# First layer of a four-layer kernel: v weights in two steps, output weights sooner, two scans in flight, norm row ahead of transposes, den steps moved

## The chip, the cores and the metric

One core of one Trainium2 chip. The metric is the device time of one execution in microseconds, the median of several runs. All runs compared here are of the fast state; the one run that fell into the slow state is named where it occurs.

## The reference

Four layers on 2048 rows of 1024 columns, in bfloat16: linear attention, gated product, and both again with the same weights. The attention layer is what the change touches.

```python
phi = lambda t: jnp.where(t > 0, t + 1, jnp.exp(t)) + 1e-6
pq, pk = phi(q), phi(k)                      # q, k, v = layernorm(x) @ wqkv, 32 heads of 32
kv  = jnp.einsum("bhsd,bhse->bhde", pk, v)
z   = jnp.einsum("bhsd->bhd", pk)
num = jnp.einsum("bhqd,bhde->bhqe", pq, kv)
den = jnp.einsum("bhqd,bhd->bhq", pq, z)[..., None] + 1e-6
...                                          # x = x + (num / den) @ wo
h   = (x @ w_gate) * (x @ w_up)              # gated layer, x = x + h @ w_down
```

## The kernel before

TensorE works almost all the time. In the first layer it makes keys, then queries interleaved with an x product (which takes the place of the v product), then folds `kv` with the output weights `wo`, and goes on to the gated layer. Beside this, ScalarE "scans" all gated-layer weights: 42 stripes of 128x2048 are fetched and their squares summed, for a scale that is needed only at the gated layer. Transfers are issued on three queues: SyncE's (transposes of the divided queries, weights of the next layer), GpSimd's (scan stripes from number 16 on) and ScalarE's (the v weights `wv` and `wo`, both 2 x 1 MB).

```python
wo = [ST[...], TX[...]]                     # both halves lie in buffers that query preparation used before
pqb = [...3 x W..., ...3 x MX...]           # six buffers for query tiles; the transpose of tile t frees one for tile t+6
def load_o():
    for n in range(2):
        nc.scalar.dma_start(out=wo[n], in_=wo_v[:, :, n * NB:(n + 1) * NB])
...
def scan_fetch():
    while scanned[1] < scanned[2]:
        i = scanned[1]
        if any(scan_buf[j] is scan_buf[i] for j in range(scanned[0], i)) or i >= max(EARLY, scanned[0] + 3):
            return
        (nc.sync if i < SYNC else nc.gpsimd).dma_start(out=scan_buf[i], in_=scan_src(i))
        scanned[1] += 1
...
def den_divide(t, pq, den):                 # last step of a query tile
    nc.vector.tensor_tensor(out=pqh, in0=pqh, in1=den..., op=ALU.mult)
    tx(pq, t, t // TPG)                     # dma_start_transpose on SyncE's queue
...
def kvo_unit(c):                            # needs wo; line 932 of the profile
    for n in range(2):
        nc.tensor.matmul(out=ps[:, n, :], lhsT=kvt[:, c, :], rhs=wo[n][:, c, :], start=True, stop=True)
    nc.scalar.activation(out=KVo[c], in_=ps, func=ACT.Copy, scale=rz[:, c:c + 1])
...
    scanned[2] = MID                        # MID = 32: from here scans up to 31 may be fetched
    scan_fetch()
    q(7, b0, 2)
    scan_step(1)
    q(8, a1, 1)
    scan_step(1)
    q(9, b1, 1)
    scan_step(1)
    q(10, b0, 2)
    load_o()
    scan_step(1)                            # scan 27, counted from 0
```

## Time and profile before

| | before |
|---|---|
| time, median of 3 runs | 1492.12 us |
| span of the profiled run | 1488.0 us |
| TensorE's waits in the first layer that the change aims at | 11.5 us |
| first matmul of the x products | 73.92 us |
| second half of `wo`: issued, landed | 165.14, 179.65 us |
| first matmul with that half | 179.70 us |
| first matmul with the sums in TX, gated layer | 256.33 us |

The rows from the fourth on are milestones: the times at which TensorE passes fixed places of the program. The difference of a milestone between two kernels tells what was won or lost up to there. The list of waits, the slow-clock stretches and the entry to the gated layer are shown in the prediction.

### The profile page before, as it was taken

The numbers are of one execution on the slowest core, as the hardware profiler recorded it, in microseconds if no ns is written. First come the engines' busy times: TensorE is split into PE (matmuls) and PEld (weight loads), VectorE is DVE, ScalarE is ACT, GpSimd is POOL, SyncE is SP. The second block draws the span as 40 slices with busy tenths as digits, with TensorE's granted clock in tenths as the row PEclk, the third lists the DMA queues.
The fourth block names the chain that finished last, engine by engine and source line by source line (L and its number), as shares of the span: only waits on it lengthen the run. The fifth ranks groups of instructions, "written<-read, shape, count | busy, mean of one in ns | idle before, by whom it ended". The sixth has DMA issues, their size and how long they took to land. (4 is left out here: it accounts for less than half of the span.)

```text
span 1488.0 us, 17649 instructions
## 1 busy us (share of the span) xinstructions
PE 1469.0 (99%) x6913; PEld 668.1 (45%) x6913; DVE 1056.5 (71%) x1577; ACT 744.5 (50%) x693; POOL 103.3 (7%) x230
## 2 busy tenths in 40 slices
PE   9899899999999999999999999999999999999999
PEld 3344444444444444444444445444444444444444
DVE  7676788988866477776479778867776845777532
ACT  6678687787700355550087347545563015566200
POOL 2201112000001000000042000200000100000000
PEclk9999999999999999999999999999999999999999
DMA  6466958697647333325739444353332753333442
GB/s 179 119 200 199 282 116 194 199 268 213 214 148 218 82 94 93 88 85 182 221 85 241 71 132 95 64 127 92 86 86 99 243 164 95 85 85 85 154 166 84
DMA packets 267443, 213.29 MB, mean 143 GB/s; under 512 B 102240, under 2 KB 250336, under 8 KB 263776
## 3 DMA queue, kind: packets, MB, share of 16 engines
q1 hardware_dynamic: 254352, 181.63, 43.3%
q0 software_dynamic: 6624, 24.12, 5.8%
q10 hardware_dynamic: 6384, 6.42, 1.3%
q8 instruction: 54, 0.88, 0.3%
q14 instruction: 29, 0.24, 0.1%
HBM read 162.59 MB, written 27.00 MB: 127 GB/s over the span
## 5 line engine op out<-in xcount | busy, mean ns | idle before, releaser
L1008 PEld LDWEIGHTS <-K 128*128 128x128 f16 x3136 | 306.8, 98 | 369.9 <-DVE TX L973 0.2
L1008 PE MATMUL Q<-XT,K 128*128 128x512 bf16 (+1 forms) x1792 | 405.7, 379 | 0.0
L1303 PE MATMUL Q<-K,K 128*128 128x512 f16 (+2 forms) x1582 | 340.4, 377 | 0.0
L1008 PE MATMUL Q<-TX,K 128*128 128x512 f16 x1344 | 308.4, 379 | 0.0
L970 ACT ACTIVATE K<-K,fac 128x2048 f16<-128x2048 bf16 x112 | 224.6, 2008 | 130.5 <-DMA K<-in_B_w_gate_dram 128.4
L1303 PEld LDWEIGHTS <-K 128*128 128x128 f16 x1582 | 154.3, 98 | 184.5
L973 DVE TENSOR_TENSOR K<-K 128x1024 f16<-128x1024 f16 (+1 forms) x244 | 157.3, 666 | 99.1 <-ACT K L970 96.5
L973 DVE TENSOR_TENSOR W<-MX,Q 128x1024 f16<-128x1024 f32 x88 | 107.4, 1220 | 37.4 <-PE Q L1008 18.6
L1028 ACT COPY MX<-Q 128x1024 f32<-128x1024 f32 x60 | 60.8, 1013 | 122.0 <-PE Q L1008 109.6
L973 DVE TENSOR_TENSOR W<-W,Q 128x1024 f16<-128x1024 f32 x80 | 97.6, 1220 | 17.7 <-PE Q L1008 13.2
L1028 ACT COPY W<-Q 128x1024 f32<-128x1024 f32 x52 | 52.6, 1012 | 89.8 <-PE Q L1008 77.3
L419 PE MATMUL Q<-K,K 128*128 128x512 bf16 x384 | 90.5, 391 | 5.1 <-DMA K<-ST 2.2
L973 DVE TENSOR_TENSOR K<-K,K 128x512 f16<-128x512 f16 (+1 forms) x148 | 87.7, 597 | 4.2
L419 PE MATMUL Q<-K,XT 128*128 128x512 bf16 x384 | 86.3, 379 | 1.0 <-DVE rz L464 0.5
L237 ACT ACTIVATE K<-K 128x2048 bf16<-128x2048 bf16 x42 | 79.9, 1907 | 5.4 <-DMA K<-in_B_w_down_dram 3.4
L1012 DVE TENSOR_TENSOR K<-W 128x512 f16<-128x512 f16 x168 | 71.3, 424 | 5.7
L1317 DVE SCALAR_TENSOR_TENSOR W<-Q,kap,X 128x1024 f32<-128x1024 f32 x16 | 20.5, 1284 | 65.7 <-PE Q L1303 65.7
L394 ACT ACTIVATE W<-Q 128x1024 bf16<-128x1024 f32 (+1 forms) x43 | 40.3, 940 | 49.4 <-PE Q L419 49.2
L297 DVE BATCH_NORM_STATS2 st<-X 128x6 f32<-128x512 bf16 x98 | 62.0, 674 | 3.0 <-DMA X<-in_A_x_dram 2.9
L1025 ACT COPY MX<-Q 128x1024 f32<-128x1024 f32 x28 | 28.3, 1009 | 70.2 <-PE Q L1008 57.3
L419 PEld LDWEIGHTS <-K 128*128 128x128 bf16 x384 | 38.0, 100 | 54.4 <-DMA K<-K 5.5
L303 POOL TENSOR_SCALAR ve<-mv 128x1 f32<-128x1 f32 x48 | 12.4, 258 | 704.9 <-DVE mv L301 704.5
(198 smaller groups left out, 1379.5 us busy)
## 6 DMA issues: line engine op xcount, KB each, us to landing
K<-WD SPq DMA_DIRECT2D x28, 1792.0 KB, 7.4
K<-in_B_w_gate_dram SPq DMA_DIRECT2D x70, 512.0 KB, 4.1
K<-in_B_w_up_dram SPq DMA_DIRECT2D x58, 512.0 KB, 5.2
K<-in_A_wqkv_dram SPq DMA_DIRECT2D x8, 1024.0 KB, 6.9
WZ<-K POOLq DMA_DIRECT2D x16, 512.0 KB, 7.0
K<-in_B_w_down_dram POOLq DMA_DIRECT2D x14, 512.0 KB, 6.9
K<-in_B_w_up_dram POOLq DMA_DIRECT2D x12, 512.0 KB, 5.0
K<-in_B_w_down_dram SPq DMA_DIRECT2D x10, 512.0 KB, 5.6
```

The lines of the kernel that those rows point to most:

```text
L237: nc.scalar.activation(out=scan_buf[i], in_=scan_buf[i], func=ACT.Square, accum_out=acc[:, m, c:c + 1])
L297: nc.vector.bn_stats(out=stat[t][0][:, c, :], in_=X[:, t, c * NB:(c + 1) * NB])
L394: nc.scalar.activation(out=e, in_=ps, func=ACT.Exp)
L419: nc.tensor.matmul(out=ps, lhsT=xt[:, k, tl * P:(tl + 1) * P], rhs=w[:, k, :], start=(k == 0), stop=(k == KD - 1))
L970: nc.scalar.activation(out=b.bitcast(F16), in_=b, func=ACT.Copy, scale=fac[:, m:m + 1])
L973: eng.tensor_tensor(out=o, in0=a, in1=b, op=op)
L1008: nc.tensor.matmul(out=pair[:, m, :], lhsT=stationary(n, p, m, k), rhs=moving[p][:, k, :], start=(p in (1, 2, 5) and k == 0), stop=(k == K ...
L1012: nc.vector.tensor_tensor(out=hA[i][:, u, :], in0=gu[:, 0, :], in1=gu[:, 1, :], op=ALU.mult)
L1025: nc.scalar.copy(out=snaps[u, 1], in_=a)
L1028: nc.scalar.copy(out=snaps[u, p], in_=a)
L1303: nc.tensor.matmul(out=ps_[:, lo:hi], lhsT=act[:, u, j * P:(j + 1) * P], rhs=w[:, u, lo:hi], start=(p in (1, 2, 5) and u == 0), stop=(u == ...
L1317: stt(out=o, in0=ps_, scalar=kap[:, 0:1], in1=x, op0=ALU.mult, op1=ALU.add)
```

## The change

Intent: take away TensorE's short waits in the first layer. The output weights are issued two query tiles sooner; the v weights come in two steps, which costs scans 18 to 23 two of their four buffers; only two scans are kept in flight; the one-column norm row is read back ahead of two transposes; and a small product (`z_column`) with its denominators is moved from query 4 to query 9.

```diff
-    scan_buf = [scan_a[i % 4] for i in range(EARLY)] + [scan_c[i % 4] for i in range(NSCAN - EARLY)]
+    scan_buf = [scan_a[i % 4 if i < 18 else 2 + i % 2] for i in range(EARLY)] + [scan_c[i % 4] for i in range(NSCAN - EARLY)]
...
-            if any(...) or i >= max(EARLY, scanned[0] + 3):
+            if any(...) or i >= max(EARLY, scanned[0] + 2):
...
-            if i in (EARLY - 3, EARLY - 1):
-                n = (i - EARLY + 3) // 2
+            if i in (18 - 1, EARLY - 1):
+                n = (i + 1) // EARLY
                 nc.scalar.dma_start(out=wv[n], in_=wqkv_v[...])
...
-        q(3, b0, 2)
+        q(3, b0, 3)
...
         q(4, a0, 3)
-        at_pair(b0)
-        z_column()
...
         q(8, a1, 1)
+        load_o()
         scan_step(1)
+        at_pair(a0)
+        z_column()
         q(9, b1, 1)
         scan_step(1)
-        q(10, b0, 2)
-        load_o()
+        q(10, b0, 1)
...
                 elif i == 3:
                     nc.sync.dma_start(out=WS[:, :], in_=part[:, 3:4])
-                elif i == 6:
+                elif i == 4:
                     nc.sync.dma_start(out=row, in_=WS[:, :].rearrange("p o -> o p").to_broadcast([P, P]))
-                elif i == 8:            # norm from the row
+                elif i == 9:
-                elif i == 9:            # key scale
+                elif i == 10:
```

More of the change, by code (lines that the diff above doesn't have):

```diff
@@ L226, in scan_fetch @@
             i = scanned[1]
-            if any(scan_buf[j] is scan_buf[i] for j in range(scanned[0], i)) or i >= max(EARLY, scanned[0] + 3):
+            if any(scan_buf[j] is scan_buf[i] for j in range(scanned[0], i)) or i >= max(EARLY, scanned[0] + 2):
                 return
```

## The prediction

> **What bounds the kernel now.** I read the page first: TensorE is busy nearly the whole span, so only its idle time and its slow-clock time can be won. The first row is TensorE's share; the second block is the list of what TensorE waited for (engine and line, releaser: us in total, times, longest).
>
> ```profile
> PE 1469.0 (99%) x6913; PEld 668.1 (45%) x6913; DVE 1056.5 (71%) x1577; ACT 744.5 (50%) x693; POOL 103.3 (7%) x230
> ...
> PE Q L932 <- DMA TX<-in_A_wo_dram: 5.3, 1, 5.3
> PE Q L419 <- DMA K<-ST: 2.2, 1, 2.2
> PE Q L419 <- ACT W L408: 1.9, 2, 1.7
> ...
> PE Q L419 <- DMA K<-K: 1.0, 2, 0.5
> ...
> PE Q L932 <- DMA ST<-in_A_wo_dram: 0.6, 1, 0.6
> ...
> PE Q L419 <- DVE rz L464: 0.5, 1, 0.5
> ```
>
> All of these lie in the first layer, and every part of the change aims at one of them. Their sum is 5.3+2.2+1.9+1.0+0.6+0.5 = 11.5 us. Then I cut the trace into one- and two-microsecond stretches around the two long ones (columns: stretch, length, busy us and count for PE, PEld, DVE, ACT, POOL; granted clock; DMA share, GB/s).
>
> ```profile
> 42.00:43.00 1.00, 1.00 (x4) 0.33 (x3) 0.00 (x0) 0.00 (x0) 0.00 (x0) 0.50 1.02 382
> ...
> 178.00:180.00 2.00, 0.30 (x1) 0.13 (x2) 1.01 (x3) 0.00 (x0) 0.00 (x0) 0.53 1.40 145
> 180.00:181.00 1.00, 1.00 (x4) 0.35 (x3) 0.00 (x0) 0.65 (x1) 0.00 (x0) 0.50 1.19 315
> ```
>
> After each long wait the clock is at half: TensorE runs 4 matmuls per us instead of 5 or more. The first slow stretch is 3.4 us (41.6 to 45.0), the second 6.8 us (178.1 to 184.9), of which TensorE works 5.2. At half speed that costs 1.7 and 2.6 us more. So the ceiling of the whole change is 11.5 + 1.7 + 2.6 = 15.8 us, 1.1% of 1492. **A gain over 2% is out of reach.**
>
> The last view is the entry to the next layer (the timeline of VectorE and TensorE there, and of ScalarE 40 us earlier; brackets are idle time and its releaser):
>
> ```profile
> 252.65 1.23 DVE L973 TENSOR_TENSOR TX<-XT,XT 128x2048 f16<-128x2048 bf16 x1 [1.80 <-DMA XT<-K]
> 252.88 3.62 PE L1008 MATMUL Q<-XT,K 128*128 128x512 bf16 x16
> ...
> 254.92 1.22 DVE L973 TENSOR_TENSOR TX<-XT,TX 128x2048 f16<-128x2048 bf16 x1
> ...
> 256.19 0.88 PEld L1008 LDWEIGHTS <-K 128*128 128x128 f16 x5 [0.20 <-DVE TX L973]
> ```
> ```profile
> 206.39 1.91 ACT L237 ACTIVATE K<-K 128x2048 bf16<-128x2048 bf16 x1
> 208.19 0.20 ACT L237 ACTIVATION_READ_ACCUMULATOR K<-K 128x1 f32 x1
> 210.47 2.00 ACT L970 ACTIVATE K<-K,fac 128x2048 f16<-128x2048 bf16 x1 [2.08 <-DVE fac L266]
> 215.92 1.91 ACT L237 ACTIVATE K<-K 128x2048 bf16<-128x2048 bf16 x1 [3.44 <-DMA K<-in_B_w_down_dram]
> ```
>
> The gated layer's third product needs the sums in TX, and already now it waits 0.20 us for them. They come from transposes of the norms that ScalarE makes after its last scan; ScalarE is busy without a gap from 215.9 to 242.5. So there is no slack there: time won earlier on TensorE counts only as far as this chain moves with it.
>
> **What the Trainium skill says.** "TensorE: Matmul & The Clock Gate", Part 1: an idle window of about 3.4 us puts the array at half clock until a busy one has passed. The trace agrees: 0.50, in stretches of 3.4 and 6.8 us. "DMA: Bandwidth & Descriptors", Queues, rings and completion order: each engine takes packets in turn from its queues, and a completion write lands only after all earlier writes of that engine. This agrees: the one-column norm store (L1191, 0.5 KB) takes 9.0 us to land, and the transpose issued behind it at 33.24 takes 7.6 instead of 3.1. Same page, Specifications: transfers below 512 B are read-modify-writes; that fits the 9.0 us for 4 B per partition. "Perfetto Trace Analysis", Tensor Engine Instruction, says that ScalarE and VectorE run strictly first in, first out: a scan that waits for its data holds all after it; the 3.44 us in front of the scan at 215.92 are such a wait.
>
> **The change, part by part.**
>
> (a) Norm row read ahead of transposes. The read (L1193) is issued at 39.65 because it waits for the store's landing, not for the transposes. Moved two places up, it makes SyncE's queue stand from 31.1 to 39.6 with the transpose for key tile 8 behind it. That transpose is then issued at about 40.05 and lands 3.1 later at 43.1 to 43.5, against 40.8 now. TensorE's 2.2 us wait becomes about 4.6 and the half clock may last a window longer: 2.4 + 0.8 = 3.2 lost. In return the row lands near 42.0 instead of 44.3 (no x loads ahead of it), tile 10's scale no longer stands behind the norm's power on GpSimd, and tile 11's statistics run on VectorE at 42.3 instead of 46.6. That gives the later tiles about 4 us of slack, so the waits for K<-K (1.0) and W L408 (1.9) should go, and some clock loss with them: 2.9 to 3.6 won. Net: **-0.4 us**, range -2 to +3.
>
> (b) v weights in two steps. Scans 18 to 23 now have two buffers. A buffer turns round in 0.5 us wait + 0.5 issue + 4 to 5 landing, plus the 1.9 us scan: two scans in about 7 us, not four. They ran at 133.98 to 150.3; I get scan 20 at 141.2 instead of 137.8 and scan 23 at about 150.6 instead of 148.4. Query exponentials behind them slip by about 2.5 us. Their PSUM pairs are next used 7 us later, so TensorE shouldn't see it, except through (d).
>
> (c) Output weights sooner. The issue at 164.7 moves two query tiles up, 2 x 3.45 = 6.9 us, to 157.8. But the second half of the v weights, on the same queue, is issued about 2 us later (152.6) and shares the engines with four 512 KB scan fetches. The loads took 9.3 and 14.5 us; beginning to move at about 162 instead of 166.9, the second lands near 174.5 against the need at 173.4. I expect a wait of 1.5 us (0 to 4) in place of 5.9, and most of the 2.6 us of clock loss gone: **-6.5 us**.
>
> (d) Den steps and the z column. The 0.5 us wait for rz goes. Its new place is followed by the kv product in the same PSUM bank, and VectorE, late by (b), may read it after 164.5: 0.8 us new. **+0.3 us**.
>
> (e) Two scans in flight. The order of the built program shows one change that matters: the fetch of scan 32 now stands in GpSimd's queue behind the power for the gate scales (which waited for VectorE until 209), and ScalarE does scan 32 before its first weight conversion. Scan 32 ran at 206.4, and the conversion at 210.5 in an idle gap. Now both come after the fetch has landed, in the stretch that is full: 1.9 + 2.0 = 3.9 us more on the chain to the gated layer.
>
> Sum: TensorE reaches the gated layer earlier by 0.4 + 6.5 - 0.3 = 6.6 us. The chain to the sums starts with VectorE's backlog, which moves earlier by about 8 (it idled 7.6 us behind the stalled query tile), then loses 3.9: it moves by about 4. TensorE then **waits about 2.6 us at L1008 for TX**, with a half-clock window in perhaps half of the runs (0.8 on average). Kernel: 4.0 less 0.8 is 3.2; I take 4, since I may have been harsh on (a). 1492.1 - 4 = 1488.
>
> **Rivals.** (1) The chain holds nothing back and all waits go: 1492 - 13 = 1479. For it: the wo wait is the largest and its issue moves the most. Against: the 0.20 us wait that stands there already, and (e) lengthens just that chain. (2) The row read costs more than it saves and wo still comes late, as the DMA engines are full from 152 to 185: same to +3, 1492 to 1495. For it: SyncE's queue stands 8.5 us. Against: issue 7 us sooner. (3) DMA becomes the bound of the scans and ScalarE's FIFO stalls TensorE at 140 to 155: +2 to +4. Against: 7 us of PSUM slack.
>
> **Range and chances.** The ceiling 1492 - 15.8 = 1476 and the rivals bound it; three runs of before differ by 4 us, so noise alone is 2. Eight in ten: 1483 to 1493. Faster by over 2% needs 30 us of an available 15.8; slower by 2% needs a new stall of 30 us.
>
> **What would show it.** Right: the wait for TX<-wo at L932 under 4 us and no 6.8 us slow stretch after it; the wait at L419 for K<-ST grown from 2.2 to 4 to 5; K<-K and L408 waits gone; ScalarE idle for some 8 us before scan 32, ended by the DMA of w_down; a new wait of 2 to 4 us at L1008 for TX L973. Wrong: the wo load still over 4 us late (contention), no wait at L1008 (the chain had slack), a store that lands well before 39.6 with nothing queued behind it, or ScalarE waits for w_up that reach TensorE.

## More of the kernel before

One more view of this kernel is needed later: the busy times around the `wo` wait, in stretches of ten microseconds (columns: stretch, length, busy us and instruction count of PE, PEld, DVE, ACT and POOL, granted clock, DMA share, GB/s).

```profile
150.00:160.00 10.00, 10.00 (x49) 4.52 (x47) 9.41 (x13) 6.01 (x8) 2.66 (x5) 1.00 0.97 330
160.00:170.00 10.00, 10.00 (x95) 6.50 (x94) 8.70 (x13) 9.70 (x11) 1.08 (x3) 1.00 1.15 246
170.00:180.00 10.00, 4.11 (x18) 1.60 (x17) 7.57 (x11) 3.92 (x4) 1.07 (x2) 0.91 1.18 290
```

Read the last two columns: the DMA engines are busy for the whole 30 us (share about 1; values above 1 occur) and move 330, 246 and 290 GB/s.

## The result and the profile after

The changed kernel took 1495.69 us (4 runs, 1494.21 to 1497.73), the kernel before 1492.8 us in the same rounds (4 runs, 1489.47 to 1494.03). The ratio is 1.0024, with a 95% interval of 1.0003 to 1.0045: a loss of some 3.6 us, where a gain of 4 was predicted. A ratio is the mean time of one kernel's fast runs over that of the other's of the same rounds, so not quite the ratio of the medians quoted.

First, what TensorE waits for in the changed kernel (engine and line, releaser: us in total, times, longest).

```profile
PE Q L932 <- DMA TX<-in_A_wo_dram: 7.4, 1, 7.4
PE Q L419 <- DMA K<-ST: 5.9, 1, 5.9
PE Q L1008 <- DVE TX L973: 1.8, 1, 1.8
...
PE Q L922 <- DVE rz L464: 1.0, 1, 1.0
...
PE Q L419 <- DVE K L746: 0.5, 1, 0.5
...
PE Q L419 <- ACT W L398: 0.2, 1, 0.2
```

The wait for `wo`, the largest aim of the change, has grown from 5.3 + 0.6 to 7.4 us although the load was issued 6.4 us sooner. The waits for K<-K and W L408 are gone as hoped, and a wait of 1.8 us at L1008 is new. Next, the load itself in both kernels: the view of the tile TX, which gives the issue (start in us at the end of the line) and the time to landing. First before, then after.

```profile
L161 ACTq DMA_DIRECT2D TX<-in_A_wo_dram x1: 595/595/595, 165.1 to 165.1; - x1
...
DMA to landing us min/median/max: 14.5/14.5/14.5
```
```profile
L161 ACTq DMA_DIRECT2D TX<-in_A_wo_dram x1: 3983/3983/3983, 158.7 to 158.7; - x1
...
DMA to landing us min/median/max: 24.9/24.9/24.9
```

It left at 158.7 instead of 165.1 and landed at 183.6 instead of 179.65. The same stretches as above for the changed kernel, and one of five microseconds behind them:

```profile
150.00:160.00 10.00, 9.41 (x51) 4.38 (x50) 9.19 (x12) 7.46 (x9) 2.35 (x4) 1.00 1.10 256
160.00:170.00 10.00, 8.99 (x87) 5.89 (x87) 8.81 (x14) 9.35 (x12) 1.61 (x3) 1.00 1.11 321
170.00:180.00 10.00, 5.95 (x30) 2.51 (x28) 5.40 (x8) 6.26 (x7) 0.54 (x1) 0.99 1.10 239
```
```profile
180.00:185.00 5.00, 1.35 (x4) 0.54 (x5) 3.19 (x5) 0.71 (x1) 0.00 (x0) 0.50 1.22 278
```

The DMA engines are as full as before; they moved 256, 321 and 239 GB/s, 272 on average against 289 before. So it isn't that more was sent: in these 30 us somewhat less got through, 8.2 million bytes against 8.7, and in another order. Last, the two places at which TensorE is held, and ScalarE ahead of scan 32 (brackets: idle time and its releaser).

```profile
44.26 6.07 PE L419 MATMUL Q<-K,K 128*128 128x512 bf16 x14 [5.93 <-DMA K<-ST]
```
```profile
175.87 0.38 PE L932 MATMUL Q<-ST,W 128*128 128x512 bf16 x1
183.65 0.61 PE L932 MATMUL Q<-TX,W 128*128 128x512 bf16 x1 [7.39 <-DMA TX<-in_A_wo_dram]
```
```profile
217.87 1.91 ACT L237 ACTIVATE K<-K 128x2048 bf16<-128x2048 bf16 x1 [8.52 <-DMA K<-in_B_w_down_dram]
219.68 0.19 ACT L237 ACTIVATION_READ_ACCUMULATOR K<-K 128x1 f32 x1
219.78 1.99 ACT L970 ACTIVATE K<-K,fac 128x2048 f16<-128x2048 bf16 x1
```
```profile
255.73 3.62 PE L1008 MATMUL Q<-XT,K 128*128 128x512 bf16 x16
261.16 1.90 PE L1008 MATMUL Q<-TX,K 128*128 128x512 f16 x8 [1.82 <-DVE TX L973]
```

The milestones give the balance of the two profiled runs. The x products start at 74.77 (0.85 later than before), the product with the second `wo` half at 183.65 (3.95 later), the product with TX at 261.16 (4.83 later), and the end comes 5.2 later (1493.2 against 1488.0). So about three quarters of what the profiled run lost was lost by 184 us.

### The profile page after: what moved, and what is told of

The parts are those of the page before. It is cut to its first block, busy times and chain, and to the rows that moved or that the text cites. A ratio compares the mean times of both kernels' runs of the same rounds, so it can differ in the third digit from the quotient of the medians.

```text
span 1493.2 us, 17555 instructions
## 1 busy us (share of the span) xinstructions
PE 1464.6 (98%) x6821; PEld 668.8 (45%) x6913; DVE 1056.5 (71%) x1577; ACT 745.3 (50%) x693; POOL 103.7 (7%) x230
## 5 line engine op out<-in xcount | busy, mean ns | idle before, releaser
L1008 PEld LDWEIGHTS <-K 128*128 128x128 f16 x3136 | 306.7, 98 | 372.0 <-DVE TX L973 2.3
L1008 PE MATMUL Q<-XT,K 128*128 128x512 bf16 (+1 forms) x1734 | 396.4, 379 | 3.1
L1008 PE MATMUL Q<-TX,K 128*128 128x512 f16 x1344 | 308.4, 379 | 1.9 <-DVE TX L973 1.8
L237 ACT ACTIVATE K<-K 128x2048 bf16<-128x2048 bf16 x42 | 79.9, 1905 | 15.5 <-DMA K<-in_B_w_down_dram 8.5
```

The source lines that it names most:

```text
L237: nc.scalar.activation(out=scan_buf[i], in_=scan_buf[i], func=ACT.Square, accum_out=acc[:, m, c:c + 1])
L1008: nc.tensor.matmul(out=pair[:, m, :], lhsT=stationary(n, p, m, k), rhs=moving[p][:, k, :], start=(p in (1, 2, 5) and k == 0), stop=(k == K ...
```

## The experiments

Eighteen kernels were run. In the expectations, T stands for the explanation that `wo` and the transposes of the queries take turns on the DMA engines, Q for the one that `wo` stands behind the late v weights in its own queue, and D for the one that the engines are simply full, of the scan fetches above all. Later expectations speak of the sharing theory: `wo` shares the engines with both, the transposes and the scan fetches.

### Undo one part at a time

Each of these is the changed kernel with one part taken back.

n_row: the row is read at step 6 again.

```diff
-                elif i == 4:
+                elif i == 6:
                     nc.sync.dma_start(out=row, ...)
```

> The changed kernel with the norm row's read back behind the transposes. If the moved read is what makes key tile 8 late: the wait for K<-ST goes from 5.9 back to about 2.2 us, the half clock after it from 6.8 to 3.4 us, the waits for K<-K (1.0) and W L408 (1.9) come back, the first x product starts at 73.9 instead of 74.8, and the kernel gains 0.9 us. Rival (the store itself landed late in that run): K<-ST stays near 5.9.

n_v: four buffers, v weights at scans 21 and 23 as before.

```diff
-    scan_buf = [scan_a[i % 4 if i < 18 else 2 + i % 2] ...
+    scan_buf = [scan_a[i % 4] ...
-            if i in (18 - 1, EARLY - 1):
+            if i in (EARLY - 3, EARLY - 1):
```

> The changed kernel with four scan buffers to the end and the v weights at scans 21 and 23, as before. Theory Q (output weights stand behind the late second v load in ScalarE's queue): v lands near 161 instead of 167, the second output load by 177, wait at L932 under 2 us, kernel 6 to 8 us faster than the changed one. Theory T (output weights are slow because they share the engines packet by packet with the transposes): the load still takes over 20 us, the wait stays over 5 us. In both, the new waits for K L746 (0.5) and rz L464 (1.0) go, as the scans no longer hold up the query exponentials: 1.5 us.

n_den: denominators and `z_column` at query 4 again, `load_o` still after query 8.

```diff
         q(4, a0, 3)
+        at_pair(b0)
+        z_column()
...
-        at_pair(a0)
-        z_column()
         q(9, b1, 1)
```

> The changed kernel with the den steps and the z column where they were; output weights still issued after query 8. Transposes of queries 4 to 7 then come in pairs near 158 and 170 again. Theory T: 3 transposes less beside the output loads, the second one takes 15 to 19 us instead of 24.9 and the wait falls from 7.4 to 0 to 3 us. Theory Q: no change of more than 1 us in its landing (183.6). The wait for rz L464 goes from 1.0 to 0.5 at the old place.

n_wo: `load_o` after query 10 again.

```diff
         q(8, a1, 1)
-        load_o()
...
         q(10, b0, 1)
+        load_o()
```

> The changed kernel with the output weights issued after query 10 again. If issuing early is what hurts (it puts them beside more transposes), the wait for TX<-wo falls below 7.4. If it helps, as intended, the wait grows by about the 6 us of the issue, to 12 to 14 us. If the queue is full anyway (theory Q, or the engines are the bound), it stays within 1 us of 7.4.

n_scan: three scans in flight again.

```diff
-            ... i >= max(EARLY, scanned[0] + 2):
+            ... i >= max(EARLY, scanned[0] + 3):
```

> The changed kernel with three scans in flight again. If the fetch of scan 32 behind GpSimd's power is what costs time at the entry to the gated layer: ScalarE's 8.5 us wait before that scan goes, the wait at L1008 for TX L973 (1.8 us) goes, kernel 1.8 us faster than the changed one. Rival (the late transposes of the queries made VectorE late there): the wait stays near 1.8 us.

| kernel | median, us | ratio to before [95%] | second `wo` half: issue, landing, us taken | TensorE's waits at L932 |
|---|---|---|---|---|
| changed | 1495.69 | 1.0024 [1.0003, 1.0045] | 158.69, 183.60, 24.9 | wo 7.4 |
| n_row | 1497.2 | 1.0052 [1.0039, 1.0065] | lands 180.39, 22.5 | wo 4.5 |
| n_v | 1493.33 | 1.0023 [1.0009, 1.0037] | 157.35, 179.78, 22.4 | wo 6.9 |
| n_den | 1501.82 | 1.0081 [1.0068, 1.0094] | lands 186.68, 27.9 | W L924 10.7 |
| n_wo | 1495.43 | 1.0034 [1.0022, 1.0046] | 165.71, 186.00, 20.3 | den 5.1, wo 3.3 |
| n_scan | 1495.07 | 1.0029 [1.0012, 1.0046] | lands 184.65, 26.8 | wo 8.9 |

No single part, taken back, makes the loss good. Five things follow.

- In every one of them `wo` takes 20 to 28 us and TensorE stands at L932 for 4.5 us or more, whatever else is different.
- n_v says that the late second half of v is not the main cause: there it landed at 160.1 instead of 167.1, and `wo` still took 22.4 us and was waited for 6.9 us. It landed 3.8 us sooner than in the changed kernel, but the time did not follow. Explanation Q, which expected a wait under 2 us, falls.
- n_scan does what part (e) of the prediction says: the wait at L1008 is gone, and ScalarE runs scan 32 without a wait, where it waited 8.5 us (it then waits 3.1 us ahead of scan 33, as the kernel before does with 3.4). The time does not follow; the wait for `wo` was 8.9 us in that run.
- n_den missed its expectation by far. It became the slowest of all: with the denominators sooner, the transposes take 12 to 22 us to land, and TensorE waits for VectorE (W L924) instead of for `wo`.
- n_wo says how little the issue decides: with `wo` issued 7 us later than in the changed kernel it landed 2.4 us later, TensorE's waits at L932 were 8.4 us instead of 7.4, and the time was the same. The wait that grows to 12 or 14 us, as the change intends it, is out. The other two forecasts (under 7.4, or within 1 of 7.4) aren't told apart: 3.3 of the 8.4 us are booked to `wo`, 5.1 to the denominators.

n_row was no faster than the changed kernel (0.9 us was expected), though its profiled run waits 3.5 us instead of 5.9 for K<-ST; the waits for W L408 (1.9) and K<-K (1.6) came back. What the row's move is worth can be read from more profiles, as all kernels are alike up to there in one way or the other. The first x product starts, with the row at step 6, at 73.92, 73.14, 74.34, 73.79 and 73.98 us (before, b_wo, n_row, b_nofetch, b_pool; mean 73.83), and with the row at step 4 at 74.77, 73.85, 74.44, 75.03, 73.54, 73.27, 73.31, 73.80 and 73.03 us (changed, n_v, n_den, n_wo, wo_sp, n_scan, no_tx, no_fetch, wo_sp1; mean 73.89). So its effect is 0.1 us with a spread of about 1, and the 0.85 us of the two profiled runs is scatter. Why n_row was timed slower stays open.

### Do one part alone: b_wo

The kernel before, with `load_o` after query 8 and nothing else.

```diff
         q(8, a1, 1)
+        load_o()
...
         q(10, b0, 2)
-        load_o()
```

> The kernel before with one edit: output weights issued after query 8 instead of 10. If the early issue alone is good, as the change intends: the second load lands at 173 to 175, wait 0 to 2 us instead of 5.3, kernel 5 to 8 us faster than before. If theory T holds for it too: issued 7 us earlier it meets the transposes of queries 4 and 5 (158 to 167) as well as 6 and 7, takes 20 us or more, and the wait stays within 2 us of 5.3.

1490.23 us, ratio 1.0000 [0.9989, 1.0012]. Here is the load, in the view of TX:

```profile
L161 ACTq DMA_DIRECT2D TX<-in_A_wo_dram x1: 595/595/595, 157.4 to 157.4; - x1
...
DMA to landing us min/median/max: 22.0/22.0/22.0
```

Issued 7.7 us sooner than before, it landed at 179.45 instead of 179.65, **0.2 us sooner**. The transposes of queries 4 and 5, issued at 157.5 and 158.9, now travel beside it; the view of their tile XT, and what VectorE waited for from 150 to 190:

```profile
L347 SPq DMA_TRANSPOSE XT<-MX x2: 1232/6541/11850, 157.5 to 158.9; - x2
...
DMA to landing us min/median/max: 17.4/19.2/21.0
```
```profile
DVE MX L401 <- DMA XT<-MX: 8.6, 2, 8.1
```
```profile
PE Q L932 <- DVE W L924: 6.0, 1, 6.0
```

Before, these two took 7.9 and 7.4 us. A transpose that has not landed keeps its MX buffer, VectorE stands 8.6 us until it may write the query tile six places on, and TensorE then waits 6.0 us for VectorE instead of 5.9 for `wo`. One crowd, another wait. This run settles that issuing sooner on the same queue gives nothing by itself, without any other part of the change.

### Which transfers make it late

no_tx: the changed kernel without the transposes of queries 4 to 7 (wrong: relative error 0.37).

```diff
-        tx(pq, t, t // TPG)
+        if not (first[0] and 4 <= t < 8):
+            tx(pq, t, t // TPG)
```

> The changed kernel without the transposes of queries 4 to 7 in the first layer; its result is wrong on purpose (stale rows there). It takes the suspected partner away. Theory T: the second output load takes 8 to 14 us from issue (24.9 in the changed kernel) and lands before 175, the wait for TX<-wo is 0 to 1 us. Rival D (the scan fetches are what it shares with): it still lands at 180 or later.

no_fetch: the changed kernel without the fetches of scans 28 to 31, which then sum what lies in their buffers (not a valid kernel).

```diff
-            (nc.sync if i < SYNC else nc.gpsimd).dma_start(out=scan_buf[i], in_=scan_src(i))
+            if not 28 <= i < 32:
+                (nc.sync if i < SYNC else nc.gpsimd).dma_start(out=scan_buf[i], in_=scan_src(i))
```

> The changed kernel without the fetches of scans 28 to 31 (issued from 160 to 173); ScalarE scans the old bytes again, so the w_down scale is off, which a power of two may or may not absorb. 2 MB less beside the output loads. Rival D: the second load takes under 15 us and the wait goes. Theory T: transposes alone keep it slow: still over 18 us, wait over 3 us. Something between says that both share.

no_both: both edits together.

> The changed kernel without the transposes of queries 4 to 7 and without the fetches of scans 28 to 31 (the result is wrong on purpose). With only the transposes gone the second output-weight tile took 18.7 us, with only these fetches gone 15.5, with both there 24.9. Sharing theory: with neither there the tile still stands behind the second half of the v weights on its queue, so it moves from about 164 and lands 8 to 11 us after its issue, at 167 to 170; no wait at L932 for it; time as without the fetches, 1483 to 1485, since no wait is left to win. Rival, a fixed delay of the queue or of the issue: landing stays at 15 us or more.

b_nofetch: the kernel *before* without the same fetches.

> The kernel before without the fetches of scans 28 to 31, output weights issued late as there. Sharing theory: the load that took 14.5 us takes 9 to 11 and lands near 175 to 176; the wait of 5.9 us at L932 falls to 1 to 3 and with it a half clock stretch; 1483 to 1487. Rival, the fetches matter only because the load was issued sooner: landing 179 to 180 and time unchanged, 1489 to 1490.

| kernel | median, us | ratio to before [95%] | second `wo` half: issue, landing, us taken | wait for `wo` |
|---|---|---|---|---|
| changed | 1495.69 | 1.0024 [1.0003, 1.0045] | 158.69, 183.60, 24.9 | 7.4 |
| no_tx | 1484.58 | 0.9962 [0.9943, 0.9981] | 159.15, 177.83, 18.7 | 2.1 |
| no_fetch | 1484.09 | 0.9958 [0.9941, 0.9976] | 158.85, 174.40, 15.5 | none |
| no_both | 1484.01 | 0.9957 [0.9939, 0.9974] | 162.03, 171.12, 9.1 | none |
| before | 1489.5 to 1492.8 | 1 | 165.14, 179.65, 14.5 | 5.9 |
| b_nofetch | 1481.18 | 0.9941 [0.9925, 0.9958] | 165.00, 173.08, 8.1 | none |

(The profiled run of no_both fell in the slow state, so its clock times are not compared; its time in the table is that of its other runs.) The views of TX, no_tx first, then no_fetch:

```profile
L161 ACTq DMA_DIRECT2D TX<-in_A_wo_dram x1: 2572/2572/2572, 159.1 to 159.1; - x1
...
DMA to landing us min/median/max: 18.7/18.7/18.7
```
```profile
L161 ACTq DMA_DIRECT2D TX<-in_A_wo_dram x1: 3385/3385/3385, 158.8 to 158.8; - x1
...
DMA to landing us min/median/max: 15.5/15.5/15.5
```

Both partners count. Without the transposes the load takes 6.2 us less, without the fetches 9.4 less, and without either 15.8 less. That is about the sum (15.6), but the 9.1 us come from the slow run and are only a hint. That no fixed delay of 15 us lies in the queue or the issue is shown by b_nofetch, a fast run, with 8.1 us. The time, however, is won only once: when the wait is gone, nothing more comes of a still earlier landing.

b_nofetch is the clearest. There the load is issued as late as before, and it lands in time all the same:

```profile
L161 ACTq DMA_DIRECT2D TX<-in_A_wo_dram x1: 595/595/595, 165.0 to 165.0; - x1
...
DMA to landing us min/median/max: 8.1/8.1/8.1
```
```profile
160.00:170.00 10.00, 10.00 (x96) 6.51 (x94) 8.84 (x13) 9.55 (x11) 0.00 (x0) 1.00 0.73 199
170.00:180.00 10.00, 10.00 (x48) 4.48 (x46) 8.22 (x13) 8.40 (x9) 0.54 (x1) 1.00 1.06 282
```

TensorE is busy for all ten microseconds from 170 to 180, at full clock, where it had 4.11 before. The gain is 8.8 us (1489.5 x 0.0059), about the wait of 5.9 and the 2.6 us that the prediction estimates for the slow clock after it. So an earlier issue was not needed for `wo` to come in time in the kernel before; four scan stripes that travel ahead of it and beside it made it late. Three of them nobody needs yet: in the trace of the kernel before, scan 28 runs at 173.7, but scans 29 to 31 only from 200.7 on.

### Another order on the queues

wo_sp: the changed kernel with the v and the output weights on SyncE's queue. wo_sp1: only the output weights.

```diff
-            nc.scalar.dma_start(out=wo[n], ...)
+            nc.sync.dma_start(out=wo[n], ...)
-                nc.scalar.dma_start(out=wv[n], ...)      # wo_sp only
+                nc.sync.dma_start(out=wv[n], ...)
```

> The changed kernel with the v and the output weights issued on SyncE's queue, the one that carries the transposes, so that their packets follow each other instead of taking turns. Theory T (packets of transposes and of weight loads in turn slow both): the second output load takes 8 to 13 us from issue instead of 24.9 and lands by 175, the wait for TX<-wo falls from 7.4 to 0 to 2 us, the transposes of queries 4 to 7 land in 3 to 9 us instead of 11 to 17, the kernel gains 7 to 9 us on the changed one. Rival D (the engines' total load is the bound, whatever the queue): the load still lands at 180 or later and the wait stays over 4 us.

> The changed kernel with the output weights alone on SyncE's queue, the v weights left on ScalarE's. With both moved it was 6 us faster than the changed kernel and the second tile took 15.6 us. If the order of the output weights and the transposes within one queue was what helped (no turns packet by packet): second tile lands at 176 to 179, wait 1 to 4 us, 1487 to 1491. If it was the move of the v weights: landing 182 to 185, wait 6 us or more, 1493 to 1496.

wo_sp took 1489.55 us, 0.9998 [0.9985, 1.0012], `wo` landed at 177.90 after 15.6 us and the wait was 2.7 us: between the forecasts of T (by 175, 0 to 2 us) and of D (180 or later, over 4 us). The same transfers on other queues landed 5.7 us sooner than in the changed kernel, so the order on the queues counts beside the total. wo_sp1 took 1491.99 us, 1.0017 [1.0002, 1.0032]; `wo` took 18.8 us and landed at 179.9, and the waits were 3.7 + 2.3. So `wo` on SyncE's queue is only part of it. Neither of the two forecasts for wo_sp1 fits fully; it lies between them, and how the gain divides isn't settled.

b_pool: the kernel before with `wo` on GpSimd's queue ahead of the fetches of scans 28 to 31, so that those stand behind it. (In the trace it stands ahead of scan 27's fetch too, which left at 153.7.)

```diff
-            nc.scalar.dma_start(out=wo[n], ...)
+            nc.gpsimd.dma_start(out=wo[n], ...)
...
         q(7, b0, 2)
+        load_o()
         scan_step(1)
```

> The kernel before with one edit: the output weights go out on GpSimd's queue just ahead of the fetch of scan 28, so that the fetches of scans 28 to 31 stand behind them on the same queue instead of sharing the engines with them. Sharing theory: the second tile lands at 168 to 172 instead of 179.7, the wait of 5.9 us at L932 and the long half clock stretch go, as without those fetches (1481.2): 1481 to 1485. Scan 28 may wait some us for its data, hidden. Rival, any sooner load is eaten by the transposes of queries 4 to 7, which then hold up VectorE as when the load alone was issued sooner on ScalarE's queue: a wait of 4 us or more at L932 for W, 1488 to 1491.

A miss, and a telling one: 1489.33 us, 0.9995 [0.9980, 1.0010]. The load came in time by far:

```profile
L161 POOL DMA_DIRECT2D TX<-in_A_wo_dram x1: 894/894/894, 152.8 to 152.8; - x1
...
DMA to landing us min/median/max: 13.4/13.4/13.4
```

It landed at 166.3, 13 us sooner than before. But the scan stripes are still to move before 180, now later and beside the transposes of queries 4 and 5, which took 17.2 and 16.6 us. VectorE and then TensorE pay:

```profile
DVE MX L401 <- DMA XT<-MX: 7.9, 1, 7.9
```
```profile
PE Q L932 <- DVE W L924: 6.9, 3, 5.8
```

The rival named in the expectation came true. The reading that fits: ordering `wo` first is of no use so long as not all that is due before 175 us gets through; then the wait falls on the transfer that comes last.

### What can be done about it

pe_sum: the kernel before, with the norm summed over partitions by a matmul with ones instead of a store to memory and a broadcast read.

```diff
-                    nc.sync.dma_start(out=WS[:, :], in_=part[:, 3:4])
...
-                    nc.sync.dma_start(out=row, ...)
+                    kps = mm_tile()
+                    nc.tensor.matmul(out=kps[:, 3:4], lhsT=ones[:], rhs=partb[:, 3:4], start=True, stop=True)
```

> The kernel before without the norm's trip through memory: the 128 partial sums are added by one matmul with ones, as the other scales are; no store, no row read. The key scale may differ in the last bit of a sum and is rounded to a power of two, so the result should hold. This measures what the store's 9 us landing costs: the wait for K<-ST (2.2) and its half clock (1.7 us lost) go, and so do VectorE's 5 us wait for the row and the waits for K<-K (1.0) and W L408 (1.9) that follow from it: the x products start at 67 to 68 instead of 73.9, kernel 5 to 7 us faster than before, if nothing later gives it back. Rival (key tile 8's own transpose and norm are as late): the start moves by under 2 us.

1488.97 us, 0.9989 [0.9976, 1.0002], so no gain clear of noise; 5 to 7 us were expected. In its profiled run it is 3.2 us ahead at the x products (70.69 against 73.92). At the `wo` wait it gives 0.9 of that back: 4.9 + 1.9 us are waited there against 5.9, and the product with the second half starts 2.3 us ahead (177.4 against 179.70). The run ended 1.9 us ahead. So the later expectation of best3, which has the lead given back at L932, holds only in part.

best1 and best2 put several of the above together: the matmul sum, v and `wo` on SyncE's queue, four scan buffers, three scans in flight, den steps as changed; best2 has the issue of `wo` still sooner in the program, ahead of query 7.

> What the runs so far point to: the changed kernel's early output weights, den steps and z column; v and output weights on SyncE's queue; four scan buffers and three scans in flight as before; the norm sum by a matmul instead of the store. x products start at about 70.7 (as with the matmul sum alone), the second output load lands by 174, wait 0 to 3 us. Theory T: 5 to 8 us faster than before, about 1483. Rival: the load still lands near 177 and the kernel stays within 2 us of before.

> As best1, but the output weights are issued as soon as their buffers are free, ahead of query 7 (about 148 instead of 157), and the transposes of queries 5 to 7 follow them in the same queue. The loads then move beside the scan fetches only: they land by 165, the wait at L932 is gone and with it the half clock, 6 to 9 us faster than before. Against: the transpose of query 5 lands at about 168 and VectorE may wait for its buffer at query 11; a new wait for DVE W L924 or L399 of 2 to 6 us at L932 would show that.

1483.77 us, 0.9960 [0.9947, 0.9973], and 1483.16 us, 0.9949 [0.9935, 0.9964]. In best2 the wait for `wo` is 0.5 us; both beat both kernels. The second half left at 157.0 in best2, not at 148 as expected, against 158.5 in best1, and landed at 172.5 instead of by 165; which of the parts bring the gain was not taken apart. best3 is pe_sum with the edit of b_pool:

> The same edit on the version whose norm is summed by a matmul (alone 1489.0, 3.2 us sooner at the x products, given back at L932). Sharing theory: both gains now reach the end, 1477 to 1481. Rival: 1485 to 1489.

1486.98 us, 0.9981 [0.9964, 0.9997], with the same kind of wait, for W L924 (5.9 us), as in b_pool (6.9): a miss that fits the same reading.

best4 is pe_sum with the fetches of scans 29 to 31 put off. The same bytes move, only later, and on SyncE's queue instead of GpSimd's.

```diff
-    EARLY, MID, SYNC = 24, 32, 16
+    EARLY, MID, SYNC = 24, 29, 16
...
-            (nc.sync if i < SYNC else nc.gpsimd).dma_start(...)
+            (nc.sync if i < SYNC or MID <= i < 32 else nc.gpsimd).dma_start(...)
...
         load_unit(0, 0)
+        if first_A:
+            scanned[2] = 32
+            scan_fetch()
         q_tile(XT_, True)
```

> The version whose norm is summed by a matmul (1489.0), with one edit: the fetches of scans 29 to 31, which are scanned only from 200 us on, leave GpSimd's queue at 162 to 170 and go out on SyncE's queue behind the first gate weights, at 178 or later. The same bytes move, only later; the output weights keep their issue. Sharing theory: as with those fetches left out, the output weights land some 9 to 11 us after their issue and the transposes of queries 4 to 7 in 4 to 6; the waits at L932 (4.9 and 1.9) fall to 2 or less; 1478 to 1483. Rival, the delay only moves the crowd on to the next loads (the gate weights, the key transposes at 190 to 201): 1486 to 1490.

1481.99 us (1480.40 to 1482.54), ratio **0.9928** [0.9911, 0.9944], correct, the best of all. TensorE's waits, the load, the put-off fetches, and the stretch around the wait:

```profile
PE Q L726 <- ACT W L409: 2.5, 1, 2.5
PE Q L932 <- DMA TX<-in_A_wo_dram: 2.1, 1, 2.1
...
PE Q L932 <- DVE W L924: 0.5, 2, 0.3
```
```profile
L161 ACTq DMA_DIRECT2D TX<-in_A_wo_dram x1: 599/599/599, 162.2 to 162.2; - x1
...
DMA to landing us min/median/max: 10.6/10.6/10.6
```
```profile
L229 SPq DMA_DIRECT2D K<-in_B_w_down_dram x3: 383/505/1539, 173.4 to 175.5; - x3
```
```profile
170.00:180.00 10.00, 7.90 (x38) 3.42 (x36) 7.39 (x11) 8.16 (x9) 0.54 (x1) 1.00 1.11 312
```

Against pe_sum the load takes 10.6 instead of 15.5 us, the waits at L932 are 2.6 instead of 7.2, no slow-clock stretch follows, and the transposes of queries 4 to 7 take 6.3 to 9.4 instead of 8.8 to 14.5 us. The put-off fetches left at 173.4 to 175.5 (not at 178 as expected) and landed by 184.9, and no new wait came of them before the gated layer, which TensorE's product with TX reaches at 246.86 (pe_sum 253.87). This shows the cause by moving work, not by taking it away. One thing is not taken apart: the three fetches also changed their queue. That the crowd and not the queue decides is argued from b_nofetch, where they are gone from GpSimd's queue and sent on none, and `wo` takes 8.1 us (10.6 here).

## Why the prediction was wrong

**The step that failed is (c), the output weights.** The prediction kept the time that the second half needs from its first movement to its landing (166.9 to 179.65 before, 12.8 us) as if it belonged to the load, let it begin at about 162, and put the landing near 174.5 and the wait at 1.5 us. Measured were a landing at 183.6, 24.9 us after the issue, and a wait of 7.4 us. So the term booked as -6.5 us was a small loss in the profiled run (TensorE resumes 3.95 us later, of which 0.85 came with it from earlier). What failed within the step is that it counted the second half of v and four scan fetches beside the load, but neither the transposes of queries 4 and 5, which the sooner load now meets, nor the scan stripes 28 to 31, which it still meets. b_wo shows it without anything else in play: 7.7 us sooner in, 0.2 us sooner out.

A sum over the bytes would have warned. Between 150 and the landing of `wo`, the kernel before has to move the second v half (1 MB), `wo` (2 MB), the stripes of scans 24 to 31 (8 x 0.5 = 4 MB) and the transposes of queries 4 to 7 (4 x 0.25 = 1 MB), together 8 MB or 8.4 million bytes, without what is issued from 174 on. At the 289 GB/s that the three stretches show, that takes 29 us: an estimate of 179, where 179.65 was measured. (The rate is taken from the very trace that it is checked against, so this says that the list is complete, and no more.) `wo` is wanted at 173.4, and by then only 6.8 million bytes can have moved. The list must be shortened by 1.6 million, or put in such an order that only what is not wanted yet is left over; issuing `wo` sooner doesn't change the sum. Leaving out scans 28 to 31 shortens it by 2.1 million bytes, 7.3 us at that rate, and the landing moved by 6.6; the closeness is partly luck, as the engines then had room (share 0.73 from 160 to 170) and the landing followed from the issue at 165.0 and the 8.1 us of the load. "DMA: Bandwidth & Descriptors" in the Trainium skill says it in the section "Issuing engines are not separate DMA queues": transfers of all issuing engines run on the same 16 DMA engines and interleave. The prediction cited the page for the turns that queues take, and did not draw this conclusion.

Bytes alone are not the whole cost, though. Here are the DMA queues of the kernel before from 150 to 180 (packets, million bytes, share of the 16 engines' time): q0 carries the scan stripes, q1 is SyncE's with the transposes, q10 carries v and `wo`. Below it is q1 from 46 to 66, where it carried five transposes and nothing else.

```profile
q0 software_dynamic: 1152, 4.19, 42.1%
q1 hardware_dynamic: 5173, 1.29, 35.5%
q10 hardware_dynamic: 3120, 3.15, 32.4%
```
```profile
q1 hardware_dynamic: 4982, 1.24, 33.9%
```

With 15% of the bytes q1 takes 32% of the busy time. Alone, 1.24 million bytes of transposes took 33.9% of 20 us, 6.8 us of all engines: 183 GB/s, where q10 comes to 324 (3.15 million bytes in 9.7 us). In direction that fits no_tx and no_fetch, where 1 MB of transposes was worth 6.2 us and 2 MB of stripes 9.4. So what it is worth to take a transfer off the list depends on its kind as well as on its bytes.

The second of its **rivals** had half of it: "wo still comes late, as the DMA engines are full from 152 to 185: same to +3, 1492 to 1495". (Its other half, that the row read costs more than it saves, did not show.) It was set aside with "issue 7 us sooner", the very argument that b_wo refutes.

Point by point, the other steps:

- (a) The mechanism came as described: SyncE's queue stood until the store had landed (38.7; 8.4 us), tile 8 came late, the wait grew to 5.9 (4.6 was predicted), and the waits for K<-K and W L408 went. Net over 14 profiles 0.1 us, -0.4 predicted: right within the scatter. (The prediction's own figures, 3.2 us lost against 2.9 to 3.6 won, give +0.3 to -0.4; it took the better end.) Its reading that the store holds up the transpose behind it is borne out by pe_sum: without the store that transpose took 3.0 us instead of 7.6.
- (b) Right. Scan 20 ran at 142.3 (141.2 predicted) and scan 23 at 151.7 (150.6), and TensorE saw little of it but what is under (d). The second v half was issued at 153.7 (152.6 predicted) and took 13.3 us, which adds to the crowd; n_v, with it sooner, is no faster in time.
- (d) The wait for rz did not go, it was 1.0 us, and 0.5 came at L746: +1.0 instead of +0.3. n_den, where this part alone is undone, is the slowest of all, as the transposes come sooner without it; but b_wo, with an early `wo` and the denominators at their old place, is no slower than the kernel before, so the part is needed only beside the others.
- (e) Right: ScalarE idles 8.5 us ahead of scan 32 ("some 8" predicted), and TensorE waits 1.8 us at L1008 (2.6 predicted), even though it arrives 2.9 us later than before. n_scan takes the wait away. It stands at 1.4 to 2.9 us in all nine fast profiles with two scans in flight, whatever `wo` does there, and in none of those with three (but for the 0.20 us that the prediction shows).
- The sum over the profiled pair: -6.6 us at the entry of the gated layer was predicted, +2.9 measured; with (e), -4 predicted and +4.8 measured; the ratio of the times says +3.6.

What stays open: whether the loss of 3.6 us belongs to (b), (c) or (e) in definite shares. The versions with one part undone lie between 1.0023 and 1.0081 and none is back at 1; their profiles move the wait about more than the parts do. What is clear is the 1.4 to 2.9 us of (e) in the profiles, and that (c) alone gained and lost nothing (b_wo, 1.0000). Part of the rest is the slow-clock windows, which fell differently from run to run (13.7 us at half clock in the first 200 us of the changed kernel's profile, 10.2 before; a wait for K<-ST of 2.0 us was followed by 3.4 us of half clock in b_nofetch, one of 2.8 us by none in n_row).

## What to carry to other kernels

Before you move a transfer forward, see whether the DMA engines have room there: add up the bytes that are due between its issue and its deadline, and divide by the GB/s that the trace shows for that kind of transfer (here 183 for transposes, 324 for weights). If they are full, issuing sooner only changes whose transfer is late, and a transpose that lands late stops an engine by keeping its buffer. Look for what in that list isn't needed yet and put that off: here three weight stripes, sent 9 to 14 us later, won 7 us (1481.99 against 1488.97; by the ratios 9, 0.9928 against 0.9989, as the two were timed in different rounds), where the five parts of the change won nothing.

## What the Trainium skill lacked or had wrong

- "DMA: Bandwidth & Descriptors", Rules for kernel authors, advises to issue a DMA early and to wait for it late. It lacks the condition: with the 16 engines full, a load issued 7.7 us sooner landed 0.2 us sooner, and two transposes beside it took 17.4 and 21.0 us instead of 7.9 and 7.4.
- No page says how much a load is stretched by other loads and transposes of the same core: the same 1 MB load took 8.1, 14.5, 22.0 and 24.9 us to land, depending on what ran beside it and ahead of it. Nor does any page give the time of a DMA transpose of this size beside other transfers: a 128x1024 tile of 2-byte elements took 3.0 us at best and 22.2 at worst.
- "DMA: Bandwidth & Descriptors", Latency and other measured facts, gives about 2 us as the fixed cost of a transfer. The store of 128 x 4 bytes took 9.0 us (before) and 8.4 us (after), with the engines 0.64 and 0.17 busy from 30 to 39 us, so a crowd does not explain it. The prediction's reading, small pieces that are read and written back, is not settled by any run; removing the store and the read of the row moved the x products 3.2 us forward.
